# Top-k attention with a capacity-limited expert layer: ScalarE's order within a step

## The chip, the core and the metric

The kernel runs on one core of a Trainium2 chip. The metric is the device time of one execution in microseconds; the kernel before has 996.05 us as the median of three runs. The engines are named as in the profile: PE is TensorE (PEld its weight loads), DVE is VectorE, ACT is ScalarE, POOL is GpSimd, SP is SyncE, which issues most of the DMAs. Each engine works through its own instructions in the order in which the program gives them; between engines, semaphores order what depends on what.

## What is computed

Attention over 8 batches and 8 heads, 576 tokens of 64 features, where each row keeps only its 32 largest scores; then an expert layer in which each token goes to its best of 8 experts and each expert takes at most 80 tokens.

```python
scores = scale * np.matmul(q, k.transpose(0, 1, 3, 2))
kth = np.partition(scores, -top_k, axis=-1)[..., -top_k:-top_k + 1]
mask = scores >= kth
scores = np.where(mask, scores, -1000000000.0)
attn = np.exp(scores - np.max(scores, axis=-1, keepdims=True))
attn = attn / (np.sum(attn, axis=-1, keepdims=True) + 1e-09)
out = np.matmul(attn, v)
...
h = np.maximum(x[tok_idx] @ w1[e], 0.0)
out[tok_idx] = gate_w[tok_idx, None] * (h @ w2[e])
```

## The kernel before

**Tiles.** The 64 heads are handled as 32 pairs of heads (n). A pair has 576 rows, cut into five tiles t0 to t4: t0 to t3 of 128 rows, and the tail t4 of 64. A tile t0 to t3 has two units, one for each head; t4 has both heads in one unit of 128 partitions. So a pair has nine units and the whole has 288 (`NU`). The 576 keys are cut in the same way into four chunks of 128 and a tail of 64.

**The way of a tile.** `front` (L219) computes a tile's scores on PE into the PSUM tile `sp`, and ACT copies them to `s` (L236). Then the 32nd largest score of each row is sought for each unit: six maxima over parts of the row (`parts`, L244), maxima and replacements over these 48 candidates (`search`, L255 and L263), on ACT a sign for each score against the 24th candidate, with a count (L260), on POOL the product `y` of scores and signs (L266), on DVE its eight largest (L268) and the pick of the threshold (L271). `below` makes the mask: units of odd number on ACT (L280), of even number on POOL (L282). `turn_w` (L302) transposes the scores on PE and adds the masks to them with matmuls: four chunks of keys of each head into the PSUM tile `ab`, and the keys' tails of both heads into the tile `cc`; ACT then takes the exponentials, first of `cc` (L325), then of `ab` (L327), into `wT`. `back` (L330) multiplies them with the values, into another part of `cc`, with the sums of the exponentials in a further column. `over` (L342) takes the reciprocals of these sums on DVE, and `divide` (L352) writes the quotients to `xn`: for t0 and t1 with one instruction on DVE (L359), for t2, t3 and t4 with two on ACT (L367).

**The rest of a pair.** `turn` (L206) transposes queries and keys of the next pair through `sp`, and ACT copies them to `both` (L217). `norm` (L369) stores `xn` to DRAM, transposes it through `sp`, copies it to `xT` (L384), multiplies it with the gate's weights into `lp` (again the PSUM tile `sp`, L389), copies that to `part` (L396) and adds it to the logits `lg` (L400).

**Buffers.** All eight banks of PSUM are taken: `sp` has four and one buffer, `ab` two and one buffer, `cc` one bank for each of two buffers. A `cc` is held from its `turn_w` until its tile has been divided.

**Order.** The order is written out by hand in `step(i)` (L455), one step for each unit. In a step come first the **letters**, a string of the instructions of the search: a letter stands for a piece of work on the unit i, i-1, i-3, i-4 or i-5. Steps of even i have two picks and two masks (`m` on ACT, `M` on POOL); every step has one sign (`e`), and, at its end, reciprocals (`z`) and divisions (`x`) of the tiles that `back` finished in the step before. After the letters comes what I call the **block T**: `turn_w` of the tile whose last unit is i-6, `front` of the tile that begins with unit i+4, `back` of the tile whose last unit is i-7 (ahead of `turn_w` if that is a tail), a `turn` if there is room, and a piece of each `norm` that is under way.

I number the steps of a pair by l, the unit of the pair that i-6 is, and write L(l) and T(l) for letters and block of that step. What T(l) has follows from the code:

| l | T(l) | divided in L(l) |
|---|---|---|
| 0 | back t4 of the pair before, `lp` and `part` | t3 of the pair before |
| 1 | turn_w t0, front t1 | t4 of the pair before |
| 2 | back t0 | |
| 3 | turn_w t1, front t2 | t0 |
| 4 | back t1, turn | |
| 5 | turn_w t2, front t3 | t1 |
| 6 | back t2, turn of `xn`, copy to `xT` | |
| 7 | turn_w t3, front t4 | t2 |
| 8 | back t3, turn_w t4, front t0 of the next pair | |

Nine is odd, so in pairs of even n the masks stand in L0, L2, L4, L6, L8, and in those of odd n in L1, L3, L5, L7.

## Time and profile before

| | |
|---|---|
| runs | 994.92, 996.05, 998.34 us (median 996.05) |
| profiled execution | 994.35 us, its span 992.5 us, granted clock 0.985 |
| 100 to 200 us: busy PE, DVE, ACT, POOL | 90.28, 94.30, 89.98, 73.09 us |
| 600 to 700 us: the same | 90.77, 94.28, 90.27, 71.43 us |
| 820 to 860 us: the same | 31.40, 26.09, 28.68, 23.97 us |
| 900 to 992 us: the same | 78.19, 10.67, 10.13, 10.33 us |
| chain that ended last | DVE 40%, PE 24%, ACT 20%, issue 9%, POOL 6%, DMA 1% |
| matmuls of turn_w that transpose into `ab` (L318) | 1148, 282 ns each |
| matmuls of back (L338) | 5760, 225 ns each |
| exponentials of `ab` (L327) and `cc` (L325) | 159 of 936 ns, 160 of 356 ns |
| signs (L260), masks on ACT (L280) | 288 of 774 ns, 144 of 777 ns |
| divisions on ACT (L367), on DVE (L359) | 128 of 306 ns and 64 for tails, 64 of 273 ns |

The attention takes the span up to some 850 us, with the same mixture of work throughout; the routing and the experts follow. A row of the profile gives how long an instruction was in its engine; instructions of one engine overlap at their ends, so the spacing of their starts is what an engine spends on each, and is shorter. A wait is put down to the instruction that came last by the profile. PE's clock was granted in full for nearly all of the attention.

### The profile page before, as it was taken

The numbers are of one execution on the slowest core, as the hardware profiler recorded it, in microseconds if no ns is written. First come the engines' busy times: TensorE is split into PE (matmuls) and PEld (weight loads), VectorE is DVE, ScalarE is ACT, GpSimd is POOL, SyncE is SP. The second block draws the span as 40 slices with busy tenths as digits, with TensorE's granted clock in tenths as the row PEclk, the third lists the DMA queues.
The fourth block names the chain that finished last, engine by engine and source line by source line (L and its number), as shares of the span: only waits on it lengthen the run. The fifth ranks groups of instructions, "written<-read, shape, count | busy, mean of one in ns | idle before, by whom it ended". The sixth has DMA issues, their size and how long they took to land.

```text
span 992.5 us, 35681 instructions
## 1 busy us (share of the span) xinstructions
PE 873.2 (88%) x13368; PEld 707.4 (71%) x13368; DVE 824.4 (83%) x4992; ACT 766.8 (77%) x1524; POOL 625.1 (63%) x474
## 2 busy tenths in 40 slices
PE   5989999898989898989898989899898988699896
PEld 3667777676767676777777777777676776578786
DVE  5899999899999999999999999999999989361010
ACT  3889989998989898989998989989898988301110
POOL 3677767776777776776677677767777777201111
PEclk9999999999999999999999999999999999879998
DMA  3454443333333232332222222211122200275910
GB/s 72 121 138 113 125 130 89 85 92 92 92 90 81 83 92 81 87 87 71 49 51 50 50 50 50 50 42 46 38 50 50 50 15 15 78 276 184 370 43 28
DMA packets 167798, 85.77 MB, mean 86 GB/s; under 512 B 117696, under 2 KB 154560, under 8 KB 167616
## 3 DMA queue, kind: packets, MB, share of 16 engines
q1 hardware_dynamic: 166592, 80.78, 29.0%
q0 software_dynamic: 1024, 2.62, 0.9%
q8 instruction: 107, 1.75, 0.7%
q14 instruction: 75, 0.61, 0.2%
HBM read 63.19 MB, written 20.19 MB: 84 GB/s over the span
## 4 chain that ended last, share of the span: by engine, by line
DVE 40%; PE 24%; ACT 20%; issue 9%; POOL 6%; DMA 1%; SPq 0%; POOLq 0%; DVEq 0%; ACTq 0%
DVE w L268 12%; DVE cand L244 11%; PE cc L338 7%; ACT sign L260 6%; DVE cand L263 4%; POOL y L266 4%; ACT wT L327 4%; PE yp L814 4%; ACT mask L280 4%; DVE top L255 3%; PE sp L229 3%; DVE pick L271 3%; ACT xn L367 3%; ACT wT L325 2%; PE ab L318 2%
## 5 line engine op out<-in xcount | busy, mean ns | idle before, releaser
L244 DVE MAX8 cand<-s 128x8 f32<-128x96 f32 x1728 | 400.1, 245 | 8.8 <-ACT s L236 8.8
L282 POOL TENSOR_SCALAR mask<-s,thr_all 128x576 bf16<-128x576 f32 x144 | 248.0, 1722 | 226.8 <-DVE pick L271 115.5
L266 POOL TENSOR_TENSOR y<-s,sign 128x576 f32<-128x576 f32 x288 | 363.2, 1282 | 13.8 <-ACT sign L260 13.8
L338 PEld LDWEIGHTS cc<-vb,wT 128*64 128x64 f32 x5760 | 181.6, 138 | 131.1 <-ACT wT L327 119.6
L338 PE MATMUL cc<-vb,wT 128*64 128x65 f32 x5760 | 203.9, 225 | 60.5 <-ACT wT L327 59.4
L268 DVE MAX8 w<-y 128x8 f32<-128x576 f32 x288 | 217.8, 756 | 13.8 <-POOL y L266 7.4
L260 ACT ACTIVATE sign<-s,w 128x576 bf16<-128x576 f32 x288 | 222.8, 774 | 1.2 <-DVE w L255 0.3
L229 PE MATMUL sp<-both 64*128 64x288 f32 (+1 forms) x1280 | 203.1, 437 | 6.4 <-ACT s L236 4.5
L236 ACT ACTIVATE s<-sp 128x1152 f32<-128x1152 f32 (+1 forms) x161 | 166.5, 1035 | 29.9 <-PE sp L229 29.4
L318 PE MATMUL ab<-ident,s 128*128 128x128 f32 x1148 | 177.5, 282 | 0.0
L327 ACT ACTIVATE wT<-ab 128x1024 f32<-128x1024 f32 (+1 forms) x159 | 148.8, 936 | 0.0
L229 PEld LDWEIGHTS sp<-both 64*128 64x128 f32 (+1 forms) x1280 | 106.0, 180 | 46.6 <-ACT s L236 7.9
L318 PEld LDWEIGHTS ab<-ident,s 128*128 128x128 f32 x1148 | 128.0, 142 | 10.1 <-issue 0.8
L255 DVE MAX8 top<-cand 128x8 f32<-128x48 f32 x576 | 115.4, 200 | 4.7
L280 ACT ACTIVATE mask<-s,thr_all 128x576 bf16<-128x576 f32 x144 | 111.9, 777 | 2.8 <-DVE pick L271 2.4
L263 DVE MATCH_REPLACE8 cand<-top,cand 128x48 f32<-128x48 f32 x576 | 110.6, 192 | 0.0
L323 PEld LDWEIGHTS <-mask 128*128 128x128 bf16 x1440 | 94.4, 98 | 1.9
L318 PE MATMUL cc<-ident,s 128*128 128x128 f32 x288 | 80.5, 279 | 8.4 <-ACT xn L367 8.4
L325 ACT ACTIVATE wT<-cc 128x256 f32<-128x256 f32 (+1 forms) x160 | 56.9, 356 | 26.3 <-PE cc L323 25.2
L217 ACT COPY both<-sp 128x1152 f32<-128x1152 f32 x31 | 34.8, 1124 | 29.7 <-PE sp L204 29.7
L826 POOL DMA_INDIRECT out_dram<-y,idx_s x8 | 7.4, 928 | 78.6 <-DVE y L825 78.6
L260 ACT ACTIVATION_READ_ACCUMULATOR sign<-s,w 128x1 f32 x288 | 56.6, 197 | 0.0
(188 smaller groups left out, 994.8 us busy)
## 6 DMA issues: line engine op xcount, KB each, us to landing
w<-in_moe_w_dram SPq DMA_DIRECT2D x10, 2048.0 KB, 12.0
w<-in_moe_w_dram SPq DMA_DIRECT2D x24, 512.0 KB, 3.9
out_dram<-zero SPq DMA_DIRECT2D x9, 1024.0 KB, 5.6
qn<-in_q_dram SPq DMA_DIRECT2D x64, 128.0 KB, 2.6
kn<-in_k_dram SPq DMA_DIRECT2D x64, 128.0 KB, 2.5
vb<-in_v_dram SPq DMA_DIRECT2D x64, 128.0 KB, 2.5
xd<-xn SPq DMA_DIRECT2D x32, 256.0 KB, 2.6
qn<-in_q_dram SPq DMA_DIRECT2D x32, 32.0 KB, 2.5
```

Source lines behind the costliest of these rows:

```text
L229: nc.tensor.matmul(o, lhsT=qT[d, t * P : t * P + m], rhs=kT[d, j * HS : (j + 1) * HS], start=True, stop=True)
L236: nc.scalar.activation(s[:, j * HS : (j + w) * HS].rearrange("p (j c) -> p j c", c=HS), ps[:, j : j + w, :HS], Act.Copy, scale=TINY)
L244: nc.vector.max(out=cand[:, j, :], in_=s[:, j * S // NG : (j + 1) * S // NG])
L260: nc.scalar.activation(sign, s, Act.Sign, bias=w9[:, 7:8], scale=-1.0, accum_out=cnt)
L263: nc.vector.match_replace(out=cand, in_to_replace=dst, in_values=cand, imm_value=LOW)
L266: nc.gpsimd.tensor_tensor(out=y, in0=s, in1=sign, op=Alu.mult)
L268: nc.vector.max(out=w9[:, 8:], in_=y)
L280: nc.scalar.activation(self.mask[i], self.s[i], Act.Relu, bias=self.thr[:, i : i + 1], scale=-1.0)
L282: nc.gpsimd.tensor_scalar(self.mask[i], self.s[i], self.thr[:, i : i + 1], None, op0=Alu.is_lt)
L318: nc.tensor.matmul(dst[h][c], lhsT=sc[:, keys[c]], rhs=ident, start=c == 0 or (c == NF and h == 0), stop=False, is_transpose=True, skip_gr ...
L327: nc.scalar.activation(wT[:, : g * NF, :], ab.rearrange("p h c r -> p (h c) r")[:, : g * NF, :], Act.Exp, scale=scale / TINY)
L338: nc.tensor.matmul(cc[r : r + TL, o], lhsT=wT[:, h * NF + c if c < NF else 2 * NF + h, r : r + TL], rhs=vb[:, c, h if t < NF else r // TL, ...
```

## The change

In `step`, the block T is put ahead of the letters. The list `done` of the tiles to be divided is still taken at the head of the step, before T adds to `drawn`, so the letters divide the tiles that `back` finished in the step before. `front` and `turn` get other special cases for the first steps. In `turn_w`, the masks of the keys' tails are added for both heads first, and then those of the four chunks. In `divide`, DVE divides t0 alone, and t1 goes to ACT with t2 to t4.

```diff
             for h in range(g):
-                mk = self.mask.pop(i + h)
-                for c in (NF, *range(NF)):
-                    nc.tensor.matmul(dst[h][c], lhsT=mk[:, keys[c]], rhs=huge if i + h in self.odd else minus, start=False, stop=True, skip_group_check=True)
+                self.mask.pop(i + h)
```
with, ahead of that loop,
```diff
+            for h, c in [(h, NF) for h in range(g)] + [(h, c) for h in range(g) for c in range(NF)]:
+                nc.tensor.matmul(dst[h][c], lhsT=self.mask[i + h][:, keys[c]], rhs=huge if i + h in self.odd else minus,
+                                 start=False, stop=True, skip_group_check=True)
```
and
```diff
-            if t < 2:
+            if t < 1:
```
and in `step`, after `first[i] = self.parts(i)`:
```diff
+                done = list(drawn)
+                drawn.clear()
+
+                def back():
+                    if whole(i - LT - 1):
+                        self.back(*units[i - LT - 1][:2])
+                        drawn.append(units[i - LT - 1][:2])
+
+                rest = whole(i - LT) and units[i - LT][2] == 2
+                if rest:
+                    back()
+                if whole(i - LT):
+                    self.turn_w(*units[i - LT][:2])
+
+                f = {0: NU, 2: 4, 3: 6}.get(i, i + 4)
+                busy = 0 <= f < NU and units[f][2] != 1
+                if busy:
+                    self.front(*units[f][:2])
+                if not rest:
+                    back()
+                if due and (not busy or i == 4) and i > 3:
+                    self.turn(due.pop())
+                    busy = True
+                for g in list(later):
...
                 for c in "GybGcGdGeGGzaxg" if i % 2 else "GGbghHmMyGcGdGeGzax":
...
                     elif c == "z":
-                        for u in drawn:
+                        for u in done:
                             self.over(*u)
                     elif c == "x":
-                        for u in drawn:
+                        for u in done:
                             self.divide(*u)
...
-                done = list(drawn)
-                drawn.clear()
...
-                f = i + 4 if i not in (0, 1) else i + 3
-                busy = 0 <= f < NU and units[f][2] != 1
-                if busy:
-                    self.front(*units[f][:2])
-                if not rest:
-                    back()
-                if due and not busy and i > 0:
-                    self.turn(due.pop())
-                    busy = True
```

## The prediction

> **What bounds the kernel now.** I read the shares of busy time first, then the waits in the stretch from 100 to 780 us, where every pair of heads repeats the same nine steps, and then the timelines of ScalarE and TensorE where one pair ends and the next begins.

> ```profile
> PE 873.2 (88%) x13368; PEld 707.4 (71%) x13368; DVE 824.4 (83%) x4992; ACT 766.8 (77%) x1524; POOL 625.1 (63%) x474
> ```
> The shares do not name a bound: three engines are near 90% in the repeating stretch. The waits there do (waiter, what it waited for: us in total, times, longest):

> ```profile
> DVE z_all L350 <- PE cc L338: 21.5, 30, 1.2
> DVE w L268 <- POOL y L266: 0.8, 2, 0.4
> ...
> PE cc L338 <- ACT wT L327: 44.1, 92, 1.0
> PE sp L389 <- ACT s L236: 13.7, 26, 0.6
> PE cc L318 <- ACT xn L367: 6.3, 13, 0.5
> ...
> ACT both L217 <- PE sp L204: 23.9, 26, 1.2
> ACT wT L325 <- PE cc L323: 17.2, 26, 1.0
> ACT s L236 <- PE sp L229: 15.8, 26, 0.6
> ```
> TensorE never waits for VectorE or GpSimd here: it works, or it waits for ScalarE. ScalarE waits for TensorE. VectorE waits for TensorE. So the pace is a loop between TensorE and ScalarE, and VectorE, though 95% busy, follows it. Two pairs take 51.97 us (starts of the first transposes into `cc` of t0: 421.69, 448.85, 473.66). TensorE's three waits, 64.1 us in 680, are 64.1 x 51.97 / 680 = **4.90 us for two pairs**; its work is the other 47.

> The third wait is what I follow. ScalarE, then TensorE, at the end of a pair:

> ```profile
> 445.84 1.13 ACT L236 ACTIVATE s<-sp 128x1152 f32<-128x1152 f32 x1 [0.58 <-PE sp L229]
> 446.87 0.77 ACT L280 ACTIVATE mask<-s,thr_all 128x576 bf16<-128x576 f32 x1
> 447.54 0.76 ACT L260 ACTIVATE sign<-s,w 128x576 bf16<-128x576 f32 x1
> 448.20 0.19 ACT L260 ACTIVATION_READ_ACCUMULATOR sign<-s,w 128x1 f32 x1
> 448.30 0.50 ACT L367 ACTIVATE xn<-cc,z_all 128x64 f32<-128x64 f32 x2
> 448.69 0.19 ACT L396 COPY part<-sp 128x40 f32<-128x40 f32 x1
> 448.76 0.79 ACT L260 ACTIVATE sign<-s,w 128x576 bf16<-128x576 f32 x1
> ```
> ```profile
> 445.72 0.80 PE L338 MATMUL cc<-vb,wT 128*64 128x65 f32 x20
> 447.02 0.76 PE L389 MATMUL sp<-wg,xT 128*64 128x8 f32 x20 [0.50 <-ACT s L236]
> 447.71 0.66 PE L318 MATMUL ab<-ident,s 128*128 128x128 f32 x4
> 448.85 0.33 PE L318 MATMUL cc<-ident,s 128*128 128x128 f32 x1 [0.48 <-ACT xn L367]
> ```
> `cc` has two buffers. The next pair's t0 takes the one of t3, so its fifth transpose cannot go before ScalarE has divided t3 (448.30). TensorE stands there with all its later work behind it: front, back, turns.

> **The parts of the change.** Durations are spacings of starts in the timeline, as an engine spends them. ScalarE: mask 0.67, sign 0.76, a tile's two divisions 0.39 (448.30 to 448.69), the tail's 0.66, `part` 0.07, exponentials 0.27 and 0.90, scores' copy 1.03 (0.54 for a tail), `both` 1.02, `xT` 0.53. TensorE: turn_w 1.80 (0.39 ahead of its first `cc`; 1.36 from there), front 1.24, back 1.32 (tail 0.68), turn 1.58, turn of `xn` 0.79, `lp` 0.69, a tail's turn_w 0.98. ScalarE to TensorE 0.16, back 0.04.

> (1) *The block T ahead of the letters L.* Nothing is added: each T comes one step earlier against the letters. But `done` is taken before T, so a tile whose back runs in T(l-1) is still divided in L(l), and T(l) now lies between. Its `cc` is held for one block more. With ScalarE's order before, from the end of front(t0) on: scores' copy, L0 (sign, division of t3), then `cc` is free; a mask in every second pair. After: scores' copy, L8 (sign), part, L0 (sign, division), with one mask in every pair, in L8 or in L0. That is 0.05 + 1.03 + 0.76 + 0.67 + 0.07 + 0.76 + 0.39 + 0.16 = 3.89 us, against TensorE's back(t4) 0.68, wait for `sp` 0.56, `lp` 0.69 and 0.39 = 2.32. **Wait 1.57 us**, where it was 0.07 (even pairs) or 0.74 (odd ones).

> (2) *Division of t1 to ScalarE*: 32 x 0.39 = 12.5 us more on ScalarE, 32 x 0.19 = 6.1 us less on VectorE (the row is 0.27 long, but the next starts 0.19 after it). VectorE's gain is worth nothing while it follows TensorE. [...]

> (3) *Tails' masks first*: the exponential of `cc` can go some 0.45 us before the last mask. It gains where ScalarE is idle at that time: at t0 alone, below.

> (4) *What else moves with T.* front and turn keep their spacing to turn_w, and front(4), front(6) come between the same letters as before. The store of `xn` (32 DMAs on SP's queue, 2.6 us to landing) is issued one letter block earlier against the letters; its buffer is written again a pair later, 25 us. Masks: a mask of the step before now stands directly ahead of T, but it is in ScalarE's own queue or was done a step earlier on GpSimd, and ten transposes (1.04 us) go first: no wait. Were VectorE behind by a step instead of ahead, each pick would show here, some 0.8 us a pair. VectorE's wait for TensorE at the reciprocals gets a whole block of slack; it is not on the path, so it goes or comes without a price.

> **The sum, walked through.** From t0's first `cc` (0), each start is the later of "TensorE free" and "ScalarE's result + 0.16". Starts of the backs, and what made TensorE wait:

> | | before, even | before, odd | after, even | after, odd |
> |---|---|---|---|---|
> | back t0 (wait) | 2.66 (0.06) | 3.33 (0.73) | 2.60 (0) | 2.60 (0) |
> | back t1 | 7.20 (0.18) | 7.72 (0.03) | 7.86 (0.90) | 7.86 (0.90) |
> | back t2 | 13.27 (0.13) | 14.44 (0.78) | 14.58 (0.78) | 13.91 (0.11) |
> | `cc` of t3 | 0 | 0 | 0 | 0.45 |
> | back t3 | 18.66 (0.29) | 20.27 (0.73) | 20.02 (0.34) | 19.41 (0) |
> | `cc` of t4 | 0 | 0 | 0 | 0.86 |
> | `lp` | 23.44 (0.56) | 25.05 (0.56) | 24.80 (0.56) | 25.05 (0.56) |
> | next `cc` of t0 | 24.59 (0.07) | 26.87 (0.74) | 27.45 (1.57) | 27.84 (1.71) |

> Row t1 after: scores' copy from 2.65, then sign, tail's division, mask, sign: 2.65 + 1.03 + 0.76 + 0.66 + 0.67 + 0.76 = 6.53, exponentials to 7.70, back at 7.86; TensorE was free at 2.60 + 1.32 + 1.80 + 1.24 = 6.96. The others go likewise. Row t4: t2 is divided only at 21.98, TensorE is there at 21.12.

> The waits before come to 4.86 us for two pairs, by the trace 4.90; the periods to 51.46, by the trace 51.97. After: 8.74 us of waits, 27.45 + 27.84 = **55.29 us**. The exponentials' waits fall nowhere but at t0 (in all 2.93 to 3.03); those for `cc` grow from 0.81 to 4.59. Two pairs cost 55.29 - 51.97 = 3.32 us more if the trace's surplus over the walk vanishes, 3.83 if it stays. Between the first t0 and the last lie 31 pairs, 15.5 times two: +51 to +59 us; the first T comes up to one step (2.75 us) earlier, so +48 to +59. I take +54. On the profiled execution's 994.35 us that is 1048; the median of the three runs is 1.7 us above it, so **1050 us**. An error of 0.3 us in each pair's one large wait is 9 us: by itself this case ranges from 1035 to 1066.

> **Rivals.** *VectorE and GpSimd set the pace (faster).* GpSimd's masks start 5.46 to 5.52 us apart in most double steps, a loop of pick, mask, y, maximum; once in two pairs 7.1 to 7.4, when a reciprocal waits for back(t4) (1.06 us at 446.6) and GpSimd's mask for TensorE to free its buffer. Both get a block of slack. The excess over 5.47 in those twelve steps is 22 us: 996 - 22 = 974, and 968 if VectorE's 6.1 us count too. For it: the chain of waits is 40% VectorE. Against: TensorE's own waits would have to shrink by 2 us in two pairs, and the walk has them grow. It decides if `cc` is free when TensorE comes to it. *No change*: what the exponentials gain the `cc` waits take, 996; needs waits near 4.9 us after. *Only ScalarE's extra work shows (slower, a little)*: 12.5 us, 1008; needs TensorE to stand at `cc` no longer than it did. *The change misses its aim*: exponentials are ahead of the signs in name, but the step before's signs still precede them; that is in the forecast.

> **Chances.** Forecast 0.71, a little slower 0.11, no change 0.04, faster 0.14. About 0.3% (3 us) can be told from nothing here. Faster 0.14, same 0.04, slower 0.82. The range reaches down to 1004 to take in the little-slower case: 1004 to 1066.

> **What would show it.** TensorE's `cc` L318 waiting for `xn` L367 about 1.6 us once in every pair (50 us in all, from 12), some 0.9 more at t4 in odd pairs; its wait for wT L327 unchanged in total; VectorE idle 5 us more in two pairs, and two pairs at 55.3 us. I am wrong if the `cc` wait stays near 0.5 us, or if ScalarE's division of t3 follows the scores' copy by less than 2 us.

## The result, and the profile after

The changed kernel takes 1079.94 us, median of four runs (1077.19 to 1081.91), against 997.19 us of the kernel before beside it: 1.083 times as long, 95% interval 1.0792 to 1.0868. The profiled execution has 1081.91 us and a span of 1080.1. Forecast were slower and 1050 us; the direction holds, and the loss of 83 us is half as large again as the 54 forecast.

Busy time in the span after:

```profile
PE 920.5 (85%) x13368; PEld 721.0 (67%) x13368; DVE 825.7 (76%) x4960; ACT 797.8 (74%) x1588; POOL 629.3 (58%) x474
```
ScalarE has 31 us more of busy time than before, VectorE 1 more, and TensorE 47 more for the same 13368 matmuls, so some of its matmuls have become slower. The rest of the loss is waiting. The waits between 100 and 780 us (waiter, what it waited for: us in total, times, longest), TensorE first:

```profile
PE cc L318 <- ACT xn L369: 54.8, 46, 1.5
PE sp L391 <- ACT s L236: 12.8, 23, 0.6
PE cc L322 <- ACT mask L280: 10.6, 22, 0.6
PE cc L340 <- ACT wT L329: 5.5, 24, 0.3
PE cc L318 <- DVE xn L361: 2.2, 11, 0.5
...
ACT wT L327 <- PE cc L322: 43.8, 58, 1.9
ACT s L236 <- PE sp L229: 31.4, 58, 1.3
...
DVE z_all L352 <- PE cc L340: 39.7, 35, 2.4
DVE w L268 <- POOL y L266: 27.6, 60, 1.2
```
TensorE's wait at `cc` for a division grew from 6.3 to 54.8 us; its wait for the exponentials fell from 44.1 to 5.5. ScalarE's waits for TensorE at the exponentials of `cc` grew from 17.2 to 43.8. VectorE's at the reciprocals did not go, but grew from 21.5 to 39.7.

The end of a pair again, ScalarE and then TensorE (start, length, line, tile):

```profile
405.37 1.13 ACT L236 ACTIVATE s<-sp 128x1152 f32<-128x1152 f32 x1 [0.64 <-PE sp L229]
406.40 0.77 ACT L280 ACTIVATE mask<-s,thr_all 128x576 bf16<-128x576 f32 x1
407.06 0.76 ACT L260 ACTIVATE sign<-s,w 128x576 bf16<-128x576 f32 x1
...
407.90 0.78 ACT L260 ACTIVATE sign<-s,w 128x576 bf16<-128x576 f32 x1
...
408.67 0.51 ACT L369 ACTIVATE xn<-cc,z_all 128x64 f32<-128x64 f32 x2
410.76 0.39 ACT L327 ACTIVATE wT<-cc 128x256 f32<-128x256 f32 x1 [1.59 <-PE cc L322]
```
```profile
407.24 0.66 PE L318 MATMUL ab<-ident,s 128*128 128x128 f32 x4
409.23 0.33 PE L318 MATMUL cc<-ident,s 128*128 128x128 f32 x1 [1.33 <-ACT xn L369]
...
411.45 2.00 PE L229 MATMUL sp<-both 64*128 64x288 f32 x8
413.38 1.39 PE L340 MATMUL cc<-vb,wT 128*64 128x65 f32 x40
414.69 0.66 PE L318 MATMUL ab<-ident,s 128*128 128x128 f32 x4
416.62 0.33 PE L318 MATMUL cc<-ident,s 128*128 128x128 f32 x1 [1.27 <-ACT xn L369]
```
This is the forecast chain: scores' copy, mask, two signs, and only then the division of t3 (408.67), for which TensorE has stood since 407.9. Two things in it were not forecast. The matmuls after the wait are slow: front's eight take 2.00 us instead of 1.24. And t1 has a wait at `cc` too (416.62, behind the tail's division).

From a first `cc` of t0 to the next it takes 27.94 us (381.29 to 409.23) and 30.01 us (409.23 to 439.24): 57.95 us for two pairs, where it was 51.97 and where the forecast had 55.29 (27.45 + 27.84).

### The profile page after: what moved, and what is told of

It is laid out like the page before. It is cut to its first block, busy times and chain, and to the rows that moved or that the text cites. A ratio compares the mean times of both kernels' runs of the same rounds, so it can differ in the third digit from the quotient of the medians.

```text
span 1080.1 us, 36009 instructions
## 1 busy us (share of the span) xinstructions
PE 920.5 (85%) x13368; PEld 721.0 (67%) x13368; DVE 825.7 (76%) x4960; ACT 797.8 (74%) x1588; POOL 629.3 (58%) x474
## 4 chain that ended last, share of the span: by engine, by line
PE 38%; ACT 29%; DVE 13%; issue 10%; POOL 6%; DMA 2%; SPq 1%; ACTq 0%; POOLq 0%; DVEq 0%
ACT sign L260 11%; PE sp L229 10%; ACT mask L280 7%; PE cc L340 5%; DVE w L268 4%; PE sp L204 4%; ACT xn L369 4%; ACT wT L329 4%; PE yp L818 3%; POOL y L266 3%; DVE cand L244 3%; PE ab L318 3%; PE ab L322 3%; PE cc L318 3%; POOL mask L282 2%
## 5 line engine op out<-in xcount | busy, mean ns | idle before, releaser
L266 POOL TENSOR_TENSOR y<-s,sign 128x576 f32<-128x576 f32 x288 | 366.1, 1282 | 94.5 <-ACT sign L260 88.1
L268 DVE MAX8 w<-y 128x8 f32<-128x576 f32 x288 | 217.8, 756 | 52.7 <-POOL y L266 46.6
L229 PE MATMUL sp<-both 64*128 64x288 f32 (+1 forms) x1280 | 218.1, 463 | 6.9 <-ACT s L236 5.0
L260 ACT ACTIVATE sign<-s,w 128x576 bf16<-128x576 f32 x288 | 220.9, 767 | 0.4
L236 ACT ACTIVATE s<-sp 128x1152 f32<-128x1152 f32 (+1 forms) x161 | 165.8, 1030 | 57.1 <-PE sp L229 53.5
L318 PE MATMUL ab<-ident,s 128*128 128x128 f32 x1148 | 182.0, 284 | 0.0
L318 PE MATMUL cc<-ident,s 128*128 128x128 f32 x288 | 86.3, 300 | 79.6 <-ACT xn L369 73.5
L229 PEld LDWEIGHTS sp<-both 64*128 64x128 f32 (+1 forms) x1280 | 113.8, 193 | 51.3 <-ACT s L236 8.3
L318 PEld LDWEIGHTS ab<-ident,s 128*128 128x128 f32 x1148 | 129.0, 142 | 10.1 <-issue 0.8
L322 PEld LDWEIGHTS <-mask 128*128 128x128 bf16 x1440 | 101.1, 104 | 27.1 <-ACT mask L280 25.1
L280 ACT ACTIVATE mask<-s,thr_all 128x576 bf16<-128x576 f32 x144 | 111.0, 771 | 0.4
L318 PEld LDWEIGHTS cc<-ident,s 128*128 128x128 f32 x288 | 41.1, 143 | 102.9 <-ACT xn L369 94.1
L327 ACT ACTIVATE wT<-cc 128x256 f32<-128x256 f32 (+1 forms) x160 | 57.2, 358 | 66.0 <-PE cc L322 65.6
L352 DVE RECIPROCAL z_all<-cc 128x2 f32<-128x2 f32 (+1 forms) x160 | 25.1, 157 | 60.9 <-PE cc L340 56.8
L369 ACT ACTIVATE xn<-cc,z_all 128x64 f32<-128x64 f32 (+1 forms) x256 | 68.2, 306 | 1.2 <-DVE z_all L352 0.8
```

The source lines that it names most:

```text
L229: nc.tensor.matmul(o, lhsT=qT[d, t * P : t * P + m], rhs=kT[d, j * HS : (j + 1) * HS], start=True, stop=True)
L236: nc.scalar.activation(s[:, j * HS : (j + w) * HS].rearrange("p (j c) -> p j c", c=HS), ps[:, j : j + w, :HS], Act.Copy, scale=TINY)
L260: nc.scalar.activation(sign, s, Act.Sign, bias=w9[:, 7:8], scale=-1.0, accum_out=cnt)
L266: nc.gpsimd.tensor_tensor(out=y, in0=s, in1=sign, op=Alu.mult)
L268: nc.vector.max(out=w9[:, 8:], in_=y)
L280: nc.scalar.activation(self.mask[i], self.s[i], Act.Relu, bias=self.thr[:, i : i + 1], scale=-1.0)
```

## The experiments

The theory: the division of a tile now stands one block T later, so each `cc` is given back later, and TensorE stands at the next tile's first `cc`. Rivals: the added work on ScalarE; or the order itself, masks and signs directly ahead of T. Times below are medians, ratios are to the kernel before in the same series (995.88, 994.05 and 994.24 us).

**The order alone.** The changed kernel with these two parts put back:
```diff
-            if t < 1:
+            if t < 2:
```
and the masks added head by head, as before.

> The block T ahead of the letters, and nothing else of the change (masks head by head, t1 divided by VectorE). Held-buffer theory (each cc is given back one block later, so TensorE stands at the first cc transposes): the order alone makes nearly the whole loss, 1060 to 1080 us, with TensorE's waits for xn at cc of 50 us or more from 100 to 780 us. Extra-work theory (ScalarE's added divisions of t1 make the loss): near 1000 us.

1071.38 us, ratio 1.0754 (1.0724 to 1.0784); TensorE waits 55.6 us at `cc` for divisions on ScalarE between 100 and 780 us.

**Everything but the order.** The kernel before with the new order of masks and `if t < 1`.

> The order of before, with the masks of the keys' tails first and t1 divided by ScalarE. Held-buffer theory: 990 to 1010 us; 12.5 us more ScalarE work at most, less what the earlier exponential of cc gives back. Extra-work theory: 1060 us or more.

1008.57 us, ratio 1.0129 (1.009 to 1.0168): 12.7 us more. Its masks are accounted for by a further run, the kernel before with nothing but the tails' masks first:

> The kernel before with the masks of the keys' tails added first, and nothing else. The exponential of cc can start some 0.45 us sooner where ScalarE is idle at that time, which before is at the tails alone; everywhere else it stands behind a sign: 992 to 997 us, not to be told from before. If the earlier exponential matters, 985 or less. The added divisions then account for all of the 12.7 us by which the change without its order was slower.

994.90 us, ratio 1.0005 (0.9988 to 1.0021). So the masks' order is worth nothing that can be measured in the order of before, and the 12.7 us are ScalarE's divisions of t1 (two instructions for each of 32 tiles), whose 32 x 0.39 = 12.5 us come through whole. Order and divisions about add up: 7.5% and 1.3%, in sum 8.8%, against 8.3% for the whole change.

**The same order, divided sooner.** In `step` of the changed kernel:
```diff
-                done = list(drawn)
-                drawn.clear()
-
                 def back():
...
+                done = list(drawn)
+                drawn.clear()
                 back = dict(a=0, b=1, c=1, d=1, e=1, y=3, g=4, h=5, m=5, H=4, M=4)
```

> The changed kernel, but the list of tiles to divide is taken after the block T instead of ahead of it, so a tile is divided in the letters of the same step as its back, directly after it. The block still comes ahead of the letters, and the masks of the step before still stand directly ahead of it. Held-buffer theory: TensorE's waits for xn at cc fall from 55 us to under 15 us (100 to 780 us), the mean granted clock is back at 0.98, and the time is 985 to 1010 us. Order theory (masks and signs of the step before directly ahead of T, and signs late for GpSimd, make the loss): above 1050 us.

1025.46 us, ratio 1.0296 (1.0266 to 1.0327): between the two. The order theory, which wanted more than 1050 us, falls as the cause of the whole loss, since block first costs 3% here and not 8%. But the expected 985 to 1010 were missed, and TensorE still waits 37.0 us. ScalarE, then TensorE, in this run:

```profile
406.11 1.13 ACT L236 ACTIVATE s<-sp 128x1152 f32<-128x1152 f32 x1 [0.64 <-PE sp L229]
407.14 0.76 ACT L260 ACTIVATE sign<-s,w 128x576 bf16<-128x576 f32 x1
...
407.89 0.51 ACT L369 ACTIVATE xn<-cc,z_all 128x64 f32<-128x64 f32 x2
```
```profile
405.93 0.80 PE L340 MATMUL cc<-vb,wT 128*64 128x65 f32 x20
...
408.46 0.33 PE L318 MATMUL cc<-ident,s 128*128 128x128 f32 x1 [1.13 <-ACT xn L369]
```
Compared with the changed kernel's timeline above, a sign and a mask less stand ahead of the division (in the other pairs it is a sign less). But `norm`, which starts when a pair's last tile is divided, has moved as well: `lp` no longer lies between the tail's back and t0, and so TensorE comes to `cc` earlier. A division behind the scores' copy is late here even with a single sign between, by the 1.13 us of this wait; in the kernel before, `lp` and its wait (0.69 and 0.50 us, at 447) lay in that time.

**One tile's division off ScalarE's queue.**
```diff
-            if t < 1:
+            if t in (0, 3):
```

> The changed kernel, with t3 divided by VectorE as t0 is, so that the cc which the next t0 takes is given back without ScalarE's queue. Held-buffer theory: t0's wait (1.54 and 1.33 us, 45 us in all) goes, and with it the low clock after it; t1's and t4's waits stay: 1015 to 1045 us. Order theory: above 1065 us.

1004.01 us, ratio 1.0079 (1.0053 to 1.0106), better than expected: the divisions of 32 tiles, moved to VectorE, give back 76 of the 83 us. TensorE's waits in this run, 100 to 780 us:

```profile
PE cc L318 <- ACT xn L369: 32.0, 38, 1.3
PE sp L391 <- ACT s L236: 14.5, 26, 0.6
PE cc L322 <- ACT mask L280: 7.1, 12, 0.6
PE cc L340 <- ACT wT L329: 5.8, 25, 0.3
```
What is left at `cc` are t1 and t4; t0 is gone from its waits, two pairs take 26.38 + 26.63 = 53.01 us, and the granted clock of that stretch is 1.00. The 4.94 us gained in two pairs are t0's waits of 1.33 and 1.54, 1.64 of slow matmuls (by the run that follows), and 0.4 besides. The run also takes work off ScalarE, 2 x 0.39 = 0.78 us in two pairs, so the wait alone isn't isolated; by this sum the work can account for 0.4 of the 4.94.

**The clock.** In `turn_w` of the changed kernel, ahead of the fifth transpose of t0's first head:
```diff
+                    if t == 0 and n > 0 and h == 0 and c == NF and not self.lean:
+                        z = zero.bitcast(BF16)
+                        for _ in range(22):
+                            nc.tensor.matmul(ab[:, 1, 0, :], lhsT=z[:, :P], rhs=z[:, :P], start=True, stop=True)
```

> The changed kernel, with 22 extra bf16 matmuls of zeros (128 x 128, into a part of ab that the transposes overwrite) between the fourth and the fifth transpose of every t0, that is, inside TensorE's wait of 1.33 to 1.54 us for cc; 22 x 0.055 = 1.2 us of work that nobody needs. Clock theory (TensorE's idle time there lets the granted clock fall, and the matmuls after it run at half speed: 1.6 us once in two pairs): few fronts longer than 1.5 us, granted clock near 1.0, 1050 to 1062 us. If the low clock costs nothing, because ScalarE is the one that is late, 1078 to 1084; if the filling itself delays cc, above 1085.

1058.76 us, ratio 1.0636 (1.0595 to 1.0677), as the clock theory has it. Work that nobody needs, put into a wait, saves some 20 us. The stretch that it fills has kept its length: from t0's first transpose to its first `cc` it is 1.99 us with the fill (396.80 to 398.79) as without (407.24 to 409.23). The stretches before, in and after such a wait (us: busy time of PE, PEld, DVE, ACT, POOL with instructions; then the granted clock, DMA share, GB/s), in the changed kernel:

```profile
405.20:409.20 4.00, 2.14 (x46) 1.74 (x44) 3.37 (x25) 3.81 (x9) 2.85 (x2) 1.00 0.34 79
409.20:413.40 4.20, 4.17 (x26) 3.17 (x26) 3.99 (x23) 1.41 (x2) 2.46 (x3) 0.59 0.23 63
413.40:417.00 3.60, 2.33 (x49) 2.02 (x48) 2.09 (x16) 3.46 (x7) 1.48 (x2) 1.00 0.00 0
...
377.00:381.20 4.20, 2.19 (x46) 1.75 (x44) 2.71 (x10) 3.88 (x9) 1.60 (x2) 1.00 0.32 74
381.20:383.90 2.70, 2.61 (x26) 2.00 (x27) 2.67 (x20) 1.45 (x3) 1.29 (x1) 1.00 0.33 98
```
TensorE is busy for about half of the 4 us up to the end of the wait, and then has a mean clock of 0.59 for 4.2 us, though it works almost without a gap. After the wait at 381.29, with the same share, the clock stays at 1.00. Over the attention, 17 fronts behind such waits take over 1.5 us, with the fill none; two pairs take 27.92 + 28.39 = 56.31 us instead of 57.95.

**Divisions of t0, t3 and the tail on VectorE.** The changed kernel with `if t in (0, 3)`, and for the tail
```diff
+                if t == NF:
+                    nc.vector.tensor_scalar(self.xn[n][:m, t, h, :], cc[p, o : o + D], self.z[p, n % NP, t, j : j + 1], None, op0=Alu.mult)
+                    continue
```

> The changed kernel with t0, t3 and the tail t4 divided by VectorE, t1 and t2 by ScalarE. Against the run that moved t3 alone (1004 us) this takes away the wait at t1's cc (0.65 and 1.26 us, which the prediction's walk left out) and 0.66 us of ScalarE's work a pair: 970 to 990 us. If t1's wait was only in the shadow of ScalarE's exponentials, it is 995 to 1004.

981.68 us, ratio 0.9863 (0.9813 to 0.9913), as expected: with the tail's division off ScalarE, TensorE's wait at `cc` for ScalarE falls from 32.0 to 7.8 us. The run can't part the wait from ScalarE's 0.66 us a pair (21 us for 32 pairs); together they are 22 us.

**All divisions on VectorE**, under the changed order and under the old one:

> The changed kernel with all five tiles divided by VectorE. No cc is then given back through ScalarE's queue: no waits of TensorE for xn beyond a few us. VectorE has some 0.8 us a pair more, in 24.7. Held-buffer theory: 960 to 985 us, the bound being VectorE with GpSimd. If the order ahead of the letters costs something of its own, above 996.

> The kernel before with all five tiles divided by VectorE; the letters still come first. ScalarE loses 1.44 us of work a pair, and t0's wait for cc (0.48 us in every second pair) goes. If the order of the change is of use once cc is given back early, this is slower than the same division with the change's order (975 to 995 here); if the order has no merit, the two are the same.

981.71 us, ratio 0.9870 (0.9832 to 0.9909), and 978.45 us, ratio 0.9831 (0.9794 to 0.9868). Both beat both kernels; between them nothing is shown, as their intervals overlap. What bounds the second, 100 to 780 us (columns as above):

```profile
100.00:780.00 680.00, 622.79 (x9191) 500.89 (x9189) 671.07 (x4186) 597.53 (x1084) 504.83 (x360) 1.00 0.28 72
```
VectorE is busy for 671 of 680 us. Two variants of this kernel followed:

> The kernel before with all tiles divided by VectorE and the masks of the keys' tails first: 975 to 980 us, the same as without the masks' order (978), since VectorE is the one that is busy without a gap; faster by 3 us or more only if TensorE's remaining waits for wT set the pace.

> The order of before with only t2 divided by ScalarE. Between all tiles on VectorE (978 us) and t1 and t2 on ScalarE: 974 to 979 if VectorE's last 0.2 us a pair matter.

977.76 us, ratio 0.9839 (0.9811 to 0.9868): the masks' order is worth nothing here either. 981.97 us, ratio 0.9871 (0.9844 to 0.9898): t2 on ScalarE gains nothing, against the 974 to 979 expected.

**The order at an equal division.** The order of before with t0, t3 and the tail on VectorE:

> The order of before with the division of labour that gave 982 us under the changed order (t0, t3, t4 by VectorE, t1, t2 by ScalarE). With cc given back early under either order, what the order itself is worth shows: 974 to 981 if the letters first are better, 982 if the order is of no account, 985 or more if the block first has a merit that the held cc hid.

987.58 us, ratio 0.9939 (0.9912 to 0.9966), against 0.9863 (0.9813 to 0.9913) with the block first. The intervals just meet, and the 0.9863 rests on two executions, so a merit of the changed order of 6 to 8 us is likely at this division and not shown; with everything on VectorE none shows.

## Why the prediction was right in direction and wrong in size

**What bounds the kernel: right.** TensorE and ScalarE set the pace and VectorE followed: it waited longer after the change, and its 6 us of lighter load bought nothing. The faster rival, VectorE and GpSimd setting the pace, came true only where the divisions left ScalarE altogether (978 us; that rival had been priced at 968 to 974).

**The held `cc` of t0: right.** 1.57 and 1.71 us were forecast (after even and after odd pairs), 1.33 and 1.54 measured. Moving t3's division to VectorE, which takes this wait away, gives back 76 us, with the slow matmuls behind the wait and up to 0.4 us in two pairs for ScalarE's lighter work in it.

**ScalarE's added divisions: right.** 12.5 us of work forecast, 12.7 us of time measured without the order. The spacing of 0.39 us for a tile's two divisions, read from the trace before, is what the runs bear out. The fastest kernels here (977.76 and 978.45 us) have every division on VectorE.

**The step that failed: the walk's sum of 55.29 us, by two terms that it left out.** Two pairs took 57.95 us.

*The larger: TensorE's durations were taken as fixed.* Front has 1.24 us in every row of the walk. It took up to 2.29 us behind the new waits, where the granted clock was 0.50 (409.61 to 413.02, for one): 57.95 - 56.31 = 1.64 us in two pairs by the fill, 25 us for 15.5 times two, about 20 in the time of the whole.

*The smaller: a wait of t1 at `cc`.* I gave the row `cc` to t3, t4 and t0 and not to t1. In odd pairs t1 takes the buffer of the tail before it, and the tail's division stands behind the scores' copy too. By the prediction's own durations it ends at 2.65 + 1.03 + 0.67 + 0.76 + 0.66 = 5.77, and with 0.16 TensorE could go at 5.93, where it arrives at 3.92 + 0.39 = 4.31. That ends turn_w of t1 at 7.29 and the front behind it at 8.53, so the back of t1 starts at 8.53 instead of 7.86: 0.67 us in two pairs, if nothing later takes it up. The trace has this wait with 1.27 us (416.62). In even pairs TensorE goes before the tail's division has ended (386.30 against 386.41), just after VectorE's division of t0, which the trace names as what it waited for (0.48 us there, 2.2 us in all); by the walk an even pair loses nothing at t1.

With t1's term the walk has 27.45 and 28.51, in sum 55.96 us; with the clock held up by the fill 27.92 and 28.39 were measured, in sum 56.31. No run takes away t1's wait alone, so the 0.67 are worked out and not isolated.

**Mis-stated, without a price.** "No wait" for masks: t1 waits up to 0.4 us and t2 up to 0.6 for ScalarE's own mask (10.6 us in all). And the exponentials' waits were to stay near 3 us in two pairs; they went, from 44.1 to 5.5 us. As I read it, TensorE is held at `cc` or at a mask shortly before and comes later to the back; that was not tested. Part of it is the order of the masks, as the order alone, with masks head by head, has 16.9 us. A wait moved up the chain is not a wait saved: two pairs are longer.

**The sum.** 5.98 us in two pairs against 3.32 to 3.83; times 15.5 that is 93 us. The profiled executions differ by 87.6: the last mask on GpSimd starts 93 us later (940.8 against 847.6), and what follows it is 5.6 us shorter. Why it is shorter was not tried. The range ended at 1066, where only errors of the walk's own terms had been allowed for; the missing term (0.67 us in two pairs) and the lower clock (1.64) both go one way.

## What to carry to other kernels

When a block is moved past another one, list every buffer that is given back in the block which now comes later, and walk all the tiles that take such a buffer, not only the one where the trace before shows a wait. An instruction that gives back a scarce buffer should not stand at the end of a queue of long ones: moving the short divisions of 32 tiles to the other engine was worth 76 us. And where the engine in question is TensorE, the matmuls behind a new wait may be priced too low at the durations seen before (front here: 1.24 us seen, up to 2.29 measured).

## What the runs showed of the hardware

A wait of 1.33 us of TensorE, with another of 0.56 us shortly before it, was followed by a mean granted clock of 0.59 over the next 4.2 us; the matmuls of front took up to 2.29 us there instead of 1.24. With the stretches cut at other times, the changed kernel's trace shows more (columns as above):
